# Retention ahead of two feed-forward layers: matmuls pinned in runs by tile form, q by chunk, one-piece decay and state update, and a first group ordered by weight tile

## The chip, the core and the metric

The kernel runs on one NeuronCore of a Trainium2 chip. The metric is the device time of one execution in microseconds, the median of three runs for the kernel before. The profiler's record of one execution (the trace) gives each engine's instructions: TensorE (PE for the matmuls, PEld for the loads of their stationary operand), VectorE (DVE), ScalarE (ACT), GpSimd (POOL) and SyncE (SP, which here only issues transfers).

## What is computed

Three stages run one after the other: a block-wise retention with a decaying state, a feed-forward layer with a mish activation, and one with elu. Input is q, k, v of shape (2, 8, 768, 64) in float32, and weights in float64.

```python
# retention, in blocks of 64 tokens (the kernel takes chunks of 128, which is the same sum)
intra = (qb @ kb.T * Dmask) @ vb               # Dmask[i, j] = lam ** (i - j) for i >= j, else 0
inter = (qb * lam_pow) @ kv_state
out   = intra + inter
kv_state = lam_block * kv_state + (kb * rev_pow).T @ vb
# layer 1: h = x @ w_in;  g = h * tanh(log(1 + exp(h)));  x = g @ w_out      (1536 tokens, 512 -> 2048 -> 512)
# layer 2: the same with g = where(h > 0, h, exp(h) - 1)
```

## The kernel before

**Retention.** The twelve chunks of 128 tokens are taken with the batch innermost: chunk n is batch n % 2, position c = n // 2. For each chunk `load` issues k, q and v on SP's queue; q comes for two chunks at once, as rows of two tokens (512 bytes), and only at even c. `transposes` turns k (four 128x128 transposes) and, at even c, q (eight) through PSUM, ACT copies them back, and GpSimd makes `q2` (q times the decay since the chunk's start) and `kd` (k times the decay to its end). `scores` multiplies k by q, per head, on half of the array's rows (64x128), the two heads of a pair into two PSUM tiles `sc`, each a buffer of its own. `decay` multiplies each by the mask `dm` on VectorE. `outputs` adds, pair by pair in `o`, one 128x128 matmul of the block-diagonal state `sbd` with `q2` (L276) and two 128x64 matmuls of v with the decayed scores (L280); then eight 128x64 matmuls make the state's increment `st` (L293), and VectorE updates `sd` in four instructions (L304). The result is split in a rounded part `xh` (ACT, L288) and a rest `xl` (VectorE, L311). The loop does transposes and scores of chunk n and then decay and outputs of chunk n-1. Each float32 matmul that is no transpose stands in the trace as two records.

**Feed-forward.** A step is (layer, group of four weight tiles, 512 tokens): `mm_in` forms h with 12 matmuls of 128x512 for each weight tile (L356), `mm_out` forms y with 12 for each of four column blocks (L398). There are 24 steps, 2304 such matmuls' worth of work in all. Each weight tile comes as float64 bits and is turned into two parts by eight VectorE instructions (L89 to L132) and one copy on ACT; a table by chunk and by unit says when. In the first group all eight tiles are made during the retention, after chunks 4 to 11. The order of units is in (step s), then out (step s-1).

**Order.** The program text gives priorities; a scheduler with a model of the times puts each engine's instructions in the order in which they are issued, and it may take a later matmul ahead of an earlier one that it believes not ready. At run time each engine keeps its order. `psH` holds two PSUM buffers for h that exist during the retention; the other buffers of the feed-forward part (`psL`, `psY`, `acc`, `g`) take the retention's memory after its end (`open_late`). The step of the first 512 tokens is written inside the retention's scope (`at_end`), so its 48 matmuls can be taken early, as far as the two buffers allow.

Of the kernel before, what the change touches and what calls it, by code (L numbers as in the profile page):

```python
# [8 lines left out]
F32 = mybir.dt.float32  # L9
# [3 lines left out]
AF = mybir.ActivationFunctionType  # L13
# [5 lines left out]
def kernel(  # L19
# [13 lines left out]
    P = 128  # L33
# [101 lines left out]

    def retention(after_chunk, at_end):
        es = ExitStack()
        cst = es.enter_context(tc.tile_pool(name="cst", bufs=1))
        io = es.enter_context(tc.tile_pool(name="io", bufs=3))
# [7 lines left out]
        nat, tr, sc, am, qT2 = {}, {}, {}, {}, {}  # L147


        def load(n, parts=1):  # L150
            b, c = chunks[n]
            for nm, src in (("k", k), ("q", q), ("v", v)):
                if nm != "q":
                    shape, rows, form = [P, H, D], slice(c * P, (c + 1) * P), "h p d -> p h d"
                elif c % 2 == 0:
                    shape, rows = [P, H, 2 * D], slice(c * P, (c + 2) * P)
                    form = "h (p x) d -> p h (x d)"
                else:
                    continue
                t = io.tile(shape, F32, tag=nm + "n", name=nm + "n", bufs=2 if nm == "q" else 3)  # L160
                for y in range(parts):
                    hs = slice(y * H // parts, (y + 1) * H // parts)
                    s = src[b, hs, rows, :]
                    nc.sync.dma_start(
                        out=t[:, hs], in_=s.rearrange(form, **({"x": 2} if nm == "q" else {}))
                    )
                nat[n, nm] = t
# [45 lines left out]
        def transposes(n):  # L213
            b, c = chunks[n]
            kn = nat[n, "k"]
            ps = psT.tile([P, PR, P], F32, tag="T", name="kTp")
            for r in range(PR):
                nc.tensor.transpose(  # L218
                    ps[:, r], kn[:, 2 * r:2 * r + 2].rearrange("p h d -> p (h d)"), ident
                )  # L220
            kT = wk.tile([P, PR, P], F32, tag="kT", name="kT")
            nc.scalar.activation(out=kT, in_=ps, func=AF.Copy)
            if c % 2 == 0:
                qn = nat[n, "q"]
                qT2[b] = wk.tile([P, PR, 2 * P], F32, tag="qT", name="qT")
                for hh in range(2):
                    ps = psT.tile([P, PR, P], F32, tag="T", name="qTp")
                    for r in range(PR):
                        nc.tensor.transpose(ps[:, r], qn[:, 2 * r + hh], ident)  # L229
                    for x in range(2):  # L230
                        dst = qT2[b][hh * D:(hh + 1) * D].rearrange("p r (i x) -> p r i x", x=2)
                        nc.scalar.activation(  # L232
                            out=dst[:, :, :, x], in_=ps[x * D:(x + 1) * D], func=AF.Copy
                        )
            qT = qT2[b][:, :, (c % 2) * P:(c % 2 + 1) * P]
            q2 = None
            if c > 0:
                q2 = wk.tile([P, PR, P], F32, tag="q2", name="q2", bufs=1)
                nc.gpsimd.tensor_tensor(out=q2, in0=qT, in1=lq, op=ALU.mult)
            kd = None  # L240
            if c < NCH - 1:
                kd = wk.tile([P, H, D], F32, tag="kd", name="kd")
                nc.gpsimd.tensor_tensor(  # L243
                    out=kd, in0=kn, in1=dm[:, :, P - 1:P].to_broadcast([P, H, D]), op=ALU.mult
                )
            tr[n] = (kT, qT, q2, kd)

        def scores(n):
            kT, qT, _, _ = tr[n]
            ps = [psS.tile([P, PR, P], F32, tag="sc", name=f"sc{hh}") for hh in range(2)]  # L250
            for r in range(PR):
                for hh in range(2):
                    rows = slice(hh * D, (hh + 1) * D)
                    nc.tensor.matmul(  # L254
                        ps[hh][:, r], lhsT=kT[rows, r], rhs=qT[rows, r], start=True, stop=True
                    )
            sc[n] = ps

        def decay(n):
            a = wk.tile([P, 2, PR, P], F32, tag="am", name="am")  # L260
            for hh, ps in enumerate(sc.pop(n)):
                nc.vector.tensor_tensor(
                    out=a[:, hh], in0=ps, in1=dm.rearrange("p (r t) i -> p r t i", t=2)[:, :, hh],
                    op=ALU.mult,
                )
            am[n] = a

        def outputs(n):
            b, c = chunks[n]
            _, _, q2, kd = tr.pop(n)  # L270
# [3 lines left out]
            for r in range(PR):  # L274
                if c > 0:
                    nc.tensor.matmul(  # L276
                        o[:, r], lhsT=sbd[b][:, r], rhs=q2[:, r], start=True, stop=False
                    )
                for hh in range(2):
                    nc.tensor.matmul(  # L280
                        o[hh * D:(hh + 1) * D, r],
                        lhsT=vn[:, 2 * r + hh],
                        rhs=a[:, hh, r],
                        start=(c == 0),
                        stop=True,
                    )
            t, col = divmod(n * P, TB)
            nc.scalar.activation(out=xh[t][:, :, col:col + P], in_=o, func=AF.Copy)  # L288
            if c < NCH - 1:
                st = psO.tile([P, PR, D], F32, tag="st", name="st")  # L290
                for r in range(PR):
                    for hh in range(2):
                        nc.tensor.matmul(  # L293
                            st[hh * D:(hh + 1) * D, r],
                            lhsT=kd[:, 2 * r + hh],
                            rhs=vn[:, 2 * r + hh],
                            start=True,
                            stop=True,
                        )
                if c == 0:  # L300
                    nc.vector.tensor_copy(sd[b], st)
                else:
                    for r in range(PR):
                        nc.vector.scalar_tensor_tensor(  # L304
                            out=sd[b][:, r], in0=sd[b][:, r], scalar=lc[:, r], in1=st[:, r],
                            op0=ALU.mult, op1=ALU.add,
                        )
# [30 lines left out]
    def open_late():  # L338
        def pool(name, **kw):
            return ctx.enter_context(tc.tile_pool(name=name, reuse_waits="tile", **kw))  # L340

        late["y"] = pool("yp", bufs=1)
        late["g"] = pool("gp", bufs=8)
# [79 lines left out]
    def mm_in_all(s):  # L423
        for i in range(G):
            h = mm_in(s, i)
            (mish, elu)[steps[s][0]](s, i, h)
            if late:
                split_g(s, i)
            weights_at(s * 2 * G + i)

    def mm_out_all(s):
        for d in range(KD):
            if s > 0:

                parts = 2 if s == NS and d == KD - 1 else 1
                for x in range(parts):
                    cols = slice(x * TB // parts, (x + 1) * TB // parts)
                    flush(s - 1, d, cols, mm_out(s - 1, d, cols))
            weights_at(s * 2 * G + G + d)
# [3 lines left out]
    CHUNKS = B * NCH  # L443
    FIRST = (4, 5, 6, 7, 8, 9, 10, 11)
    LATER = (0, 3, 6, 9, 12, 14, 16, 20)
    at = {}
    for n in range(NW):
        g, i = divmod(n, PG)
        at.setdefault(FIRST[i] - CHUNKS if g == 0 else LATER[i] + (g - 1) * 24, []).append(n)

    def weights_at(u):
        for n in at.get(u, ()):
            if n == 0:
                for m in range(AHEAD):
                    w_load(m)
            w_guard(n)
            w_bits(n)
            w_split(n)
            w_load(n + AHEAD)

    retention(lambda n: weights_at(n - CHUNKS), lambda: mm_in_all(0))
    open_late()
    for i in range(G):
        split_g(0, i)
    for s in range(NS + 1):
        if 0 < s < NS:
            mm_in_all(s)
        mm_out_all(s)
# [32 lines left out]
```

## Time and profile before

| what | us |
|---|---|
| median of three runs | 616.55 (616.34 to 617.07) |
| the profiled execution, its time | 617.07 |
| the profiled execution, its span (first to last instruction) | 615.3 |
| PE busy | 605.3 |
| VectorE busy | 446.6 |
| ScalarE busy | 227.7 |
| GpSimd busy | 172.1 |

The span is what the trace shows; 1.8 us of the execution's time lie around it. A busy time is the union of an engine's instructions, whose ends are modelled on PE; how fast PE goes is read from the distance between the starts of its instructions, not from the busy share.

### The profile page before, as it was taken

The numbers are of one execution on the slowest core, as the hardware profiler recorded it, in microseconds if no ns is written. First come the engines' busy times: TensorE is split into PE (matmuls) and PEld (weight loads), VectorE is DVE, ScalarE is ACT, GpSimd is POOL, SyncE is SP. The second block draws the span as 40 slices with busy tenths as digits, with TensorE's granted clock in tenths as the row PEclk, the third lists the DMA queues.
The fourth block names the chain that finished last, engine by engine and source line by source line (L and its number), as shares of the span: only waits on it lengthen the run. The fifth ranks groups of instructions, "written<-read, shape, count | busy, mean of one in ns | idle before, by whom it ended". The sixth has DMA issues, their size and how long they took to land.

```text
span 615.3 us, 7925 instructions
## 1 busy us (share of the span) xinstructions
PE 605.3 (98%) x3036; PEld 495.6 (81%) x3036; DVE 446.6 (73%) x751; ACT 227.7 (37%) x387; POOL 172.1 (28%) x126
## 2 busy tenths in 40 slices
PE   6999999999999999999999999999999999999997
PEld 4877777788888888888888888888888888888886
DVE  5798996499906993499549995899569965952222
ACT  3464732431323233223233534533343443254130
POOL 5143411730333143123313123213311421232130
PEclk9999999999999999999999999999999999999999
DMA  8985433023300321033202221132203320000112
GB/s 200 266 219 139 122 118 103 2 68 103 102 1 15 105 90 67 1 102 93 79 1 68 69 74 64 35 103 68 69 12 93 103 68 1 0 2 0 69 39 99
DMA packets 54807, 46.66 MB, mean 76 GB/s; under 512 B 26480, under 2 KB 49264, under 8 KB 54768
## 3 DMA queue, kind: packets, MB, share of 16 engines
q1 hardware_dynamic: 54624, 46.14, 25.6%
q8 instruction: 24, 0.39, 0.3%
q14 instruction: 15, 0.12, 0.1%
q10 hardware_dynamic: 144, 0.00, 0.0%
HBM read 43.00 MB, written 3.15 MB: 75 GB/s over the span
## 4 chain that ended last, share of the span: by engine, by line
PE 96%; DVE 1%; ACT 1%; DMA 0%; issue 0%; POOL 0%; ACTq 0%
PE y L398 42%; PE h L356 42%; PE sc L254 4%; PE o L280 3%; PE o L276 2%; PE st L293 1%; PE kTp L218 1%; PE qTp L229 1%; DMA lam_b<-in_lam_dram 0%; ACT qT L232 0%; DVE dm L187 0%; ACT L374 0%; DVE m L89 0%; POOL kd L243 0%; DVE step L185 0%
## 5 line engine op out<-in xcount | busy, mean ns | idle before, releaser
L356 PE MATMUL h<-xh,w 128*128 128x512 f32 x768 | 241.6, 390 | 0.7 <-ACT xh L288 0.7
L366 POOL TENSOR_TENSOR g<-g,g 128x512 fp32r<-128x512 f32 x96 | 137.5, 1438 | 351.9 <-ACT g L365 332.2
L356 PEld LDWEIGHTS h<-xh,w 128*128 128x128 f32 x768 | 143.8, 188 | 30.8 <-ACT xh L288 0.9
L356 PE MATMUL h<-xl,w 128*128 128x512 f32 x384 | 149.6, 389 | 0.0
L398 PE MATMUL y<-g,w 128*128 128x512 f32 x576 | 132.7, 389 | 0.0
L398 PE MATMUL y<-w,g 128*128 128x512 f32 (+1 forms) x588 | 132.5, 385 | 0.0
L398 PEld LDWEIGHTS y<-w,g 128*128 128x128 f32 x588 | 108.9, 188 | 22.0
L398 PEld LDWEIGHTS y<-g,w 128*128 128x128 f32 x576 | 108.1, 188 | 22.6 <-ACT g L365 0.2
L410 DVE TENSOR_TENSOR acc<-acc,y 128x512 f32<-128x512 f32 (+1 forms) x73 | 48.7, 673 | 75.3 <-PE y L398 75.3
L131 ACT ACTIVATE w<-m 128x512 fp32r<-128x512 f32 x64 | 40.5, 633 | 166.9 <-DVE m L120 114.3
L356 PEld LDWEIGHTS h<-xl,w 128*128 128x128 f32 x384 | 72.1, 188 | 14.8
L365 ACT ACTIVATE g<-g 128x512 fp32r<-128x512 f32 x96 | 60.0, 631 | 52.9 <-DVE g L383 51.5
L383 DVE SCALAR_TENSOR_TENSOR g<-e,h 128x512 f32<-128x512 f32 x48 | 32.7, 682 | 41.5 <-ACT e L381 26.9
L132 DVE TENSOR_TENSOR w<-m,w 128x512 fp32r<-128x512 f32 x64 | 45.7, 715 | 20.5 <-ACT w L131 20.3
L116 DVE SCALAR_TENSOR_TENSOR u<-raw,u 128x512 f32<-128x512 uint32 x64 | 57.2, 894 | 0.3
L108 DVE SCALAR_TENSOR_TENSOR b<-raw,b 128x512 int32<-128x512 int32 x64 | 50.0, 781 | 0.6
L120 DVE TENSOR_TENSOR m<-b,u 128x512 f32<-128x512 f32 x64 | 48.3, 754 | 0.3
L374 ACT ACTIVATE g<-h 128x512 f32<-128x512 f32 x48 | 28.1, 588 | 41.7 <-PE h L356 28.6
L104 DVE TENSOR_SCALAR b<-m 128x512 int32<-128x512 int32 x64 | 38.9, 609 | 0.3
L380 ACT ACTIVATE e<-h 128x512 f32<-128x512 f32 x48 | 28.2, 587 | 29.1 <-PE h L356 29.1
L112 DVE TENSOR_SCALAR u<-b 128x512 int32<-128x512 int32 x64 | 36.5, 570 | 0.3
L93 DVE TENSOR_SCALAR m<-m 128x512 f32<-128x512 f32 x64 | 35.7, 558 | 0.3
(44 smaller groups left out, 367.5 us busy)
## 6 DMA issues: line engine op xcount, KB each, us to landing
raw<-in_moe_w_in_dram SPq DMA_DIRECT2D x32, 512.0 KB, 3.7
raw<-in_moe_w_out_dram SPq DMA_DIRECT2D x32, 512.0 KB, 3.3
kn<-in_k_dram SPq DMA_DIRECT2D x11, 256.0 KB, 4.6
vn<-in_v_dram SPq DMA_DIRECT2D x11, 256.0 KB, 3.8
out_dram<-acc SPq DMA_DIRECT2D x11, 256.0 KB, 2.0
qn<-in_q_dram SPq DMA_DIRECT2D x5, 512.0 KB, 5.8
qn<-in_q_dram SPq DMA_DIRECT2D x2, 256.0 KB, 3.9
kn<-in_k_dram SPq DMA_DIRECT2D x2, 128.0 KB, 3.2
```

Source lines behind the costliest of these rows:

```text
L104: nc.vector.tensor_scalar(out=b, in0=m, scalar1=3, scalar2=0x3FFFFFF8, op0=ALU.logical_shift_left, op1=ALU.bitwise_and,)
L108: nc.vector.scalar_tensor_tensor(out=b, in0=hw, scalar=-0x40000000, in1=b, op0=ALU.bitwise_and, op1=ALU.bitwise_or)
L112: nc.vector.tensor_scalar(out=u, in0=b, scalar1=-0x800000, scalar2=None, op0=ALU.bitwise_and)
L116: nc.vector.scalar_tensor_tensor(out=u.bitcast(F32), in0=lw, scalar=2.0 ** -52, in1=u.bitcast(F32), op0=ALU.mult, op1=ALU.mult,)
L120: nc.vector.tensor_tensor(out=m.bitcast(F32), in0=b.bitcast(F32), in1=u.bitcast(F32), op=ALU.add)
L131: nc.scalar.activation(out=w[:, 0], in_=f, func=AF.Copy)
L132: nc.vector.tensor_tensor(out=w[:, 1], in0=f, in1=w[:, 0].bitcast(F32), op=ALU.subtract)
L356: nc.tensor.matmul(h, lhsT=lt, rhs=rt, start=(kk == 0 and n == 0), stop=(kk == KD - 1 and n == 2),)
L365: nc.scalar.activation(out=gg[:, 0], in_=g, func=AF.Copy)
L366: nc.gpsimd.tensor_tensor(out=gg[:, 1], in0=g, in1=gg[:, 0].bitcast(F32), op=ALU.subtract)
L398: nc.tensor.matmul(y, lhsT=lt, rhs=rt, start=(i == 0 and n == 0), stop=(i == G - 1 and n == 2),)
L410: nc.vector.tensor_tensor(out=dst, in0=dst, in1=y, op=ALU.add)
```

## The change

- The matmuls and transposes of the retention are pinned: each is kept behind the matmul written before it. The loop now does, for chunk n: load of n+3, transposes of n+1, scores of n, decay of n, outputs and state of n-1.
- q is loaded for each chunk like k (rows of 256 bytes), transposed in four transposes and copied back by one ACT instruction; k, q and v have four buffers instead of two or three.
- The two score tiles become one tile over two PSUM banks, with one buffer, and `decay` is one VectorE instruction over 1024 columns.
- In `outputs` the state's term is made by two 128x64 matmuls for a pair of heads instead of one 128x128, all of them ahead of the eight with v.
- The state update is two VectorE instructions instead of four.
- The first group goes by weight tile over all three blocks of 512 tokens (12 units "in", then out of step 0 and 1, then as before). Two of its units stand in the retention's scope. Only three weight tiles are made during the retention; the others follow in units 0 to 8, the second group's in units 10 to 24. The first four weight loads are issued after chunks 3, 5, 7 and 9. The buffers of g go from 8 to 12.

```diff
-        psS = es.enter_context(tc.tile_pool(name="psS", bufs=2, space=PSUM))
+        psS = es.enter_context(tc.tile_pool(name="psS", bufs=1, space=PSUM))
+        def pe(ins):
+            tc.keep_in_program_order(ins)
...
-                t = io.tile(shape, F32, tag=nm + "n", name=nm + "n", bufs=2 if nm == "q" else 3)
+                t = io.tile([P, H, D], F32, tag=nm + "n", name=nm + "n")
...
-            ps = [psS.tile([P, PR, P], F32, tag="sc", name=f"sc{hh}") for hh in range(2)]
+            ps = psS.tile([P, 2, PR, P], F32, tag="sc", name="sc")
...
-            for hh, ps in enumerate(sc.pop(n)):
-                nc.vector.tensor_tensor(
-                    out=a[:, hh], in0=ps, in1=dm.rearrange("p (r t) i -> p r t i", t=2)[:, :, hh],
-                    op=ALU.mult,
-                )
+            nc.vector.tensor_tensor(
+                out=a, in0=sc.pop(n), in1=dm.rearrange("p (r t) i -> p t r i", t=2), op=ALU.mult
+            )
...
+            if c > 0:
+                terms += [
+                    (r, hh, sbd[b][:, r, hh * D:(hh + 1) * D], q2[:, r])
+                    for r in range(PR) for hh in range(2)
+                ]
+            terms += [
+                (r, hh, vn[:, 2 * r + hh], a[:, hh, r]) for r in range(PR) for hh in range(2)
+            ]
+            for x, (r, hh, lt, rt) in enumerate(terms):
+                pe(nc.tensor.matmul(
+                    o[hh * D:(hh + 1) * D, r], lhsT=lt, rhs=rt,
+                    start=x < 2, stop=x >= len(terms) - 2, skip_group_check=True,
+                ))
...
-                    for r in range(PR):
-                        nc.vector.scalar_tensor_tensor(
-                            out=sd[b][:, r], in0=sd[b][:, r], scalar=lc[:, r], in1=st[:, r],
-                            op0=ALU.mult, op1=ALU.add,
-                        )
+                    nc.vector.tensor_tensor(
+                        out=sd[b], in0=sd[b], in1=lc.to_broadcast([P, PR, D]), op=ALU.mult
+                    )
+                    nc.vector.tensor_tensor(out=sd[b], in0=sd[b], in1=st, op=ALU.add)
...
+        transposes(0)
         for n in range(NC + 1):
+            load(n + 3)
+            if n + 1 < NC:
+                transposes(n + 1)
             if n < NC:
-                transposes(n)
-                if 0 < n and n + 2 < NC:
-                    load(n + 2)
                 scores(n)
+                decay(n)
             if n > 0:
-                decay(n - 1)
                 outputs(n - 1)
-                after_chunk(n - 1)
+            after_chunk(n)
...
+    seq = [("in", t, i) for i in range(G) for t in range(NTB)]
+    tail = [("out", 0), ("out", 1)]
+    for s in range(NTB, NS):
+        tail += [("in", s), ("out", s - 1)]
...
-    FIRST = (4, 5, 6, 7, 8, 9, 10, 11)
-    LATER = (0, 3, 6, 9, 12, 14, 16, 20)
+    FIRST = (4 - CHUNKS, 7 - CHUNKS, 10 - CHUNKS, 0, 2, 4, 6, 8)
+    SECOND = (10, 12, 14, 16, 18, 20, 22, 24)
+    LATER = (24, 27, 30, 33, 36, 38, 40, 44)
...
+    LOAD = {3 - CHUNKS: 0, 5 - CHUNKS: 1, 7 - CHUNKS: 2, 9 - CHUNKS: 3}
...
+    EARLY = 2
```

## Rows read from the trace of the kernel before

**Rows 1.** The page's chain that ended last: shares of the span by line.
```profile
PE y L398 42%; PE h L356 42%; PE sc L254 4%; PE o L280 3%; PE o L276 2%; PE st L293 1%; PE kTp L218 1%; PE qTp L229 1%; DMA lam_b<-in_lam_dram 0%; ACT qT L232 0%; DVE dm L187 0%; ACT L374 0%; DVE m L89 0%; POOL kd L243 0%; DVE step L185 0%
```

**Rows 2.** Windows: busy us (instructions) by engine, granted clock, DMA share, GB/s.
```profile
4.00:20.70 16.70, 15.02 (x88) 11.62 (x88) 9.25 (x16) 7.84 (x14) 5.60 (x6) 1.00 1.05 265
20.70:110.20 89.50, 89.32 (x729) 68.82 (x728) 77.98 (x158) 39.72 (x70) 25.53 (x15) 1.00 0.54 147
...
111.00:616.00 505.00, 500.84 (x2220) 415.01 (x2220) 358.88 (x576) 178.10 (x301) 137.53 (x96) 1.00 0.18 57
...
200.00:300.00 100.00, 100.00 (x443) 82.84 (x442) 81.81 (x135) 29.05 (x50) 25.61 (x17) 1.00 0.25 77
```

**Rows 3.** The same for L356 alone: PE, PEld, clock, DMA.
```profile
0.00:110.20 110.20, 24.02 (x96) 17.42 (x96) 1.00 0.62 163
```

**Rows 4.** Timeline of PE (start, us, line), the feed-forward's start and end.
```profile
110.85 0.73 PE L356 MATMUL h<-xh,w 128*128 128x512 f32 x2 [0.70 <-ACT xh L288]
...
597.70 14.14 PE L398 MATMUL y<-w,g 128*128 128x512 f32 x73
```

**Rows 5.** Timeline of PE, one chunk in the middle of the retention.
```profile
55.67 0.49 PE L276 MATMUL o<-q,sbd 128*128 128x128 f32 x2
56.09 0.44 PE L280 MATMUL o<-am,vn 128*64 128x128 f32 x4
56.46 0.49 PE L276 MATMUL o<-q,sbd 128*128 128x128 f32 x2
...
58.03 1.16 PE L254 MATMUL sc<-qT,kT 64*128 64x128 f32 x16
59.12 0.69 PE L293 MATMUL st<-vn,kd 128*64 128x64 f32 x16
59.74 1.09 PE L229 MATMUL qTp<-ident,qn 128*128 128x128 f32 x8
60.59 0.47 PE L356 MATMUL h<-xh,w 128*128 128x512 f32 x1
```

**Rows 6.** Timeline of PE, scores of one chunk in two halves.
```profile
48.96 1.16 PE L254 MATMUL sc<-qT,kT 64*128 64x128 f32 x8
50.05 0.69 PE L293 MATMUL st<-vn,kd 128*64 128x64 f32 x16
50.66 1.16 PE L254 MATMUL sc<-qT,kT 64*128 64x128 f32 x8
```

**Rows 7.** Timeline of PE, a long run of 128x64 matmuls.
```profile
27.47 1.09 PE L280 MATMUL o<-am,vn 128*64 128x128 f32 x14
28.49 0.66 PE L218 MATMUL kTp<-ident,kn 128*128 128x128 f32 x4
```

**Rows 8.** Timeline of PE, half-runs of scores early and later.
```profile
10.00 2.07 PE L254 MATMUL sc<-qT,kT 64*128 64x128 f32 x8
...
20.73 1.16 PE L254 MATMUL sc<-qT,kT 64*128 64x128 f32 x8
```

**Rows 9.** Groups of instructions to 110.2 us, VectorE: busy, mean ns, idle before.
```profile
L262 DVE TENSOR_TENSOR am<-sc,dm 128x512 f32<-128x512 f32 x24 | 16.2, 680 | 4.9 <-PE sc L254 4.9
...
L304 DVE SCALAR_TENSOR_TENSOR sd<-sd,lq,st 128x64 f32<-128x64 f32 x32 | 6.7, 268 | 0.0
```

**Rows 10.** Timeline of VectorE: a weight instruction beside GpSimd, and a 256-column one.
```profile
118.28 1.40 DVE L89 TENSOR_SCALAR m<-raw 128x512 int32<-128x512 int32 x1
...
610.44 0.42 DVE L410 TENSOR_TENSOR acc<-acc,y 128x256 f32<-128x256 f32 x1 [0.74 <-PE y L398]
```

**Rows 11.** Groups to 123 us, ScalarE and GpSimd.
```profile
L239 POOL TENSOR_TENSOR q<-qT,lq 128x512 f32<-128x512 f32 x10 | 19.5, 1955 | 49.9 <-PE o L276 49.1 <-DVE lq L202 0.7
L243 POOL TENSOR_TENSOR kd<-kn,dm 128x512 f32<-128x512 f32 x10 | 11.4, 1148 | 19.6 <-DMA kn<-in_k_dram 8.2 <-PE st L293 6.6 <-DVE lq L202 3.7
...
L288 ACT ACTIVATE xh<-o 128x512 fp32r<-128x512 f32 x12 | 7.2, 598 | 14.3 <-PE o L280 14.1
```

**Rows 12.** Transfers from 3 to 12 us: packets and rate.
```profile
DMA packets 6742, 2.21 MB, mean 245 GB/s; under 512 B 4694, under 2 KB 6742, under 8 KB 6742
```

More of the change, by code (lines that the diff above doesn't have):

```diff
@@ L146, in retention @@
         NC = len(chunks)
-        nat, tr, sc, am, qT2 = {}, {}, {}, {}, {}
+        nat, tr, sc, am, qkd = {}, {}, {}, {}, {}
+        def pe(ins):
+            tc.keep_in_program_order(ins)
         def load(n, parts=1):
+            if n >= NC:
+                return
             b, c = chunks[n]
             for nm, src in (("k", k), ("q", q), ("v", v)):
[L153 to L159, printed above, removed]
-                t = io.tile(shape, F32, tag=nm + "n", name=nm + "n", bufs=2 if nm == "q" else 3)
-                for y in range(parts):
-                    hs = slice(y * H // parts, (y + 1) * H // parts)
-                    s = src[b, hs, rows, :]
+                t = io.tile([P, H, D], F32, tag=nm + "n", name=nm + "n")
+                np_ = 1 if nm == "v" else parts
+                for y in range(np_):
+                    hs = slice(y * H // np_, (y + 1) * H // np_)
                     nc.sync.dma_start(
-                        out=t[:, hs], in_=s.rearrange(form, **({"x": 2} if nm == "q" else {}))
+                        out=t[:, hs],
+                        in_=src[b, hs, c * P:(c + 1) * P, :].rearrange("h p d -> p h d"),
                     )
@@ L235, in transposes @@
[L235 to L244, printed above, removed]
-                )
@@ L246, in transposes @@
-            tr[n] = (kT, qT, q2, kd)
+            out = []
+            for nm in ("k", "q"):
+                x = nat[n, nm]
+                ps = psT.tile([P, PR, P], F32, tag="T", name=nm + "Tp")
+                for r in range(PR):
+                    pe(nc.tensor.transpose(
+                        ps[:, r], x[:, 2 * r:2 * r + 2].rearrange("p h d -> p (h d)"), ident
+                    ))
+                t = wk.tile([P, PR, P], F32, tag=nm + "T", name=nm + "T")
+                nc.scalar.activation(out=t, in_=ps, func=AF.Copy)
+                out.append(t)
@@ new lines, in transposes @@
+            tr[n] = out
+            q2 = kd = None
+            if c > 0:
+                q2 = wk.tile([P, PR, P], F32, tag="q2", name="q2")
+                nc.gpsimd.tensor_tensor(out=q2, in0=out[1], in1=lq, op=ALU.mult)
+            if c < NCH - 1:
+                kd = wk.tile([P, H, D], F32, tag="kd", name="kd", bufs=3)
+                nc.gpsimd.tensor_tensor(
+                    out=kd, in0=nat[n, "k"], in1=dm[:, :, P - 1:P].to_broadcast([P, H, D]),
+                    op=ALU.mult,
+                )
@@ L253, in scores @@
                     rows = slice(hh * D, (hh + 1) * D)
-                    nc.tensor.matmul(
-                        ps[hh][:, r], lhsT=kT[rows, r], rhs=qT[rows, r], start=True, stop=True
-                    )
+                    pe(nc.tensor.matmul(
+                        ps[:, hh, r], lhsT=kT[rows, r], rhs=qT[rows, r], start=True, stop=True
+                    ))
             sc[n] = ps
@@ L273, in outputs @@
             o = psO.tile([P, PR, P], F32, tag="o", name="o")
[L274 to L286, printed above, removed]
+            terms = []
+            if c > 0:
+                terms += [
[6 more added lines that the diff above has]
+            for x, (r, hh, lt, rt) in enumerate(terms):
+                pe(nc.tensor.matmul(
+                    o[hh * D:(hh + 1) * D, r], lhsT=lt, rhs=rt,
+                    start=x < 2, stop=x >= len(terms) - 2, skip_group_check=True,
+                ))
             t, col = divmod(n * P, TB)
@@ L292, in outputs @@
                     for hh in range(2):
-                        nc.tensor.matmul(
+                        pe(nc.tensor.matmul(
                             st[hh * D:(hh + 1) * D, r],
@@ L342, in open_late @@
         late["y"] = pool("yp", bufs=1)
-        late["g"] = pool("gp", bufs=8)
+        late["g"] = pool("gp", bufs=12)
         late["psH"] = pool("psL", bufs=2, space=PSUM)
@@ L421, in flush, with unit @@
             nc.sync.dma_start(out=out[r0:r0 + P, cols], in_=dst)
[L423 to L426, printed above, removed]
-            if late:
[L428 to L443, printed above, removed]
-    FIRST = (4, 5, 6, 7, 8, 9, 10, 11)
-    LATER = (0, 3, 6, 9, 12, 14, 16, 20)
+    seq = [("in", t, i) for i in range(G) for t in range(NTB)]
+    HEAD = len(seq)
+    tail = [("out", 0), ("out", 1)]
+    for s in range(NTB, NS):
+        tail += [("in", s), ("out", s - 1)]
+    tail.append(("out", NS - 1))
+    for kind, s in tail:
+        seq += [(kind, s, x) for x in range(G if kind == "in" else KD)]
+    def unit(u):
+        kind, s, x = seq[u]
+        if kind == "in":
+            (mish, elu)[steps[s][0]](s, x, mm_in(s, x))
+            if late:
+                split_g(s, x)
+        else:
+            parts = 2 if u == len(seq) - 1 else 1
+            for y in range(parts):
+                cols = slice(y * TB // parts, (y + 1) * TB // parts)
+                flush(s, x, cols, mm_out(s, x, cols))
+    CHUNKS = B * NCH + 1
     at = {}
+    FIRST = (4 - CHUNKS, 7 - CHUNKS, 10 - CHUNKS, 0, 2, 4, 6, 8)
+    SECOND = (10, 12, 14, 16, 18, 20, 22, 24)
+    LATER = (24, 27, 30, 33, 36, 38, 40, 44)
     for n in range(NW):
         g, i = divmod(n, PG)
-        at.setdefault(FIRST[i] - CHUNKS if g == 0 else LATER[i] + (g - 1) * 24, []).append(n)
+        u = (FIRST, SECOND)[g][i] if g < 2 else LATER[i] + (g - 2) * 24
+        at.setdefault(u, []).append(n)
+    LOAD = {3 - CHUNKS: 0, 5 - CHUNKS: 1, 7 - CHUNKS: 2, 9 - CHUNKS: 3}
     def weights_at(u):
+        if u in LOAD:
+            w_load(LOAD[u])
         for n in at.get(u, ()):
-            if n == 0:
-                for m in range(AHEAD):
-                    w_load(m)
             w_guard(n)
@@ L459, in weights_at, with first_units @@
             w_load(n + AHEAD)
-    retention(lambda n: weights_at(n - CHUNKS), lambda: mm_in_all(0))
-    open_late()
[L463 to L468, printed above, removed]
+    EARLY = 2
+    def first_units():
+        for u in range(EARLY):
+            unit(u)
+            weights_at(u)
+    retention(lambda n: weights_at(n - CHUNKS), first_units)
+    open_late()
+    for u in range(EARLY):
+        split_g(seq[u][1], seq[u][2])
+    for u in range(EARLY, len(seq)):
+        unit(u)
+        weights_at(u)
 _INS = ["q", "k", "v", "lam", "moe_w_in", "moe_w_out", "moe2_w_in", "moe2_w_out"]
```

29 lines of the change are left out of this document (5 added, 24 removed).

## The prediction

> **What bounds the kernel now.** I read the chain that ended last first: its lines on PE add up to 96% of the span [rows 1]. So TensorE's own order of work is the clock of this kernel, and other engines count only where they make it wait. The windows split it [rows 2]: from 111.0 us on PE does nothing but the feed-forward layers. Their last matmul ends at 597.70 + 14.14 = 611.84 us [rows 4], so 500.84 us hold 2220 records, of which 24 are halves (the last block is split in two): 2208 whole ones, **0.2268 us** each. By 110.2 us 96 others were done [rows 3], 2304 in all: 2304 x 0.2268 = 522.6 us is feed-forward work that the change keeps. The other 611.84 - 522.6 = **89.2 us** are the start, the retention and its stalls. The change can only win there, and can lose there or where the first group of weights is late.
>
> That these 89 us are PE's work, not waiting, is seen in the same windows: from 20.7 to 110.2 us PE is busy 89.32 of 89.50 us, VectorE 77.98 [rows 2]. Busy on PE is modelled, so I price runs by the distance of their starts.
>
> **The change part by part, on PE.** All prices are of one chunk, from 20.7 us on. Before that a run of 8 score records takes 2.07 us, from then on 1.16 [rows 8]: the lower of TensorE's levels (1.2 GHz) and then the higher (2.4 GHz), though the granted-clock column prints 1.00 for both [rows 2].
>
> Outputs. A pair of heads takes 56.46 - 55.67 = 0.79 us before (one state matmul, two of v, thus two changes of form), four pairs 3.14 us [rows 5]. A long run of 14 records of 128x64 takes 28.49 - 27.47 = 1.02 us, four of them 56.46 - 56.09 = 0.37 [rows 5, 7]: (1.02 - 0.37)/10 = 0.065 us a record and 0.37 - 4 x 0.065 = 0.11 us for the change of form. After: 16 records for the state and 16 for v in one form, 32 x 0.065 + 0.11 = **2.19 us**, 0.95 less, in ten chunks.
>
> Scores. The scheduler issues one head of each pair (8 records) apart from the other: 50.05 - 48.96 = 1.09 us, twice a chunk [rows 6]; where both stand together, 16 records take 59.12 - 58.03 = 1.09 us as well [rows 5]. Two halves of the rows work at once if they are neighbours in the order. One tile and pinning make them neighbours: **1.09 us** a chunk. Seven of twelve chunks were split (14 runs of 8 stand alone in the timeline).
>
> State and transposes. 16 state records take 59.74 - 59.12 = 0.62 us; behind the outputs there is no change of form, so 0.62 - 0.11 = **0.51**. Eight transposes take 60.59 - 59.74 = **0.85** [rows 5]; k and q now stand together in each chunk.
>
> Sum: 2.19 + 1.09 + 0.51 + 0.85 = 4.64 us a chunk, 55.7 for twelve; the two first chunks have no state term (16 x 0.065 = 1.04 each), the two last no state update (0.51 each): **52.6 us** at the higher level.
>
> Start. The first transposes wait for k at 4 us as before. q's first half is 128 KB instead of 256, so I let PE be dense from 7.5 us and the clock rise at 20.7 as before (1 us either way). By then 0.85 + (20.7 - 7.5)/2 = 7.4 us of the 52.6 are done; the retention ends at 20.7 + 45.2 = **66 us** without stalls.
>
> **What can make PE wait.** The two units in the retention's scope (24 matmuls) may fill holes, but the pinned ones can no longer change places, so each late input now costs.
>
> Scores need the one score buffer free: the wait is behind `decay`, one VectorE instruction of 1024 columns. From 256 columns (0.42) and 512 (0.68) [rows 9, 10] it is about 0.68 + 2 x 0.26 = 1.20 us; meanwhile PE has outputs, state and transposes, 3.55 us. Outputs need `o` free: `xh` on ACT 0.60 [rows 11], then `xl` on VectorE 0.68 by the same width, maybe behind a weight instruction that GpSimd holds up, 1.40 [rows 10]: 2.7 us, against 0.51 + 0.85 + 1.09 = 2.45 us of other work. So 0 to 0.25 us, eleven times, and a little more where the scheduler's order on VectorE is unlucky: bounds 0 to 6, I take **2 us**, near the lower, since only three weight tiles lie in this stretch.
>
> VectorE's own edits cost PE nothing: the decay 1.20 instead of 2 x 0.68, the state 2 x 0.42 instead of 4 x 0.268 [rows 9, 10]; if GpSimd holds the new SBUF multiply, up to 1.40, a chunk's 2.9 us of VectorE work still fits in 4.64. ACT loses four half copies per two chunks and gains one whole one per chunk. GpSimd has 1.96 + 1.15 = 3.1 us a chunk [rows 11], also under 4.64.
>
> Loads. On SP the load of v for chunk n+3 now waits for the state matmuls of chunk n-1, and k and q of n+4 and a weight load are queued behind it; their user, the transposes of n+4, comes two rounds (9 us) later. The first four weight loads are spread over chunks 3 to 9 instead of standing in one block in the first 20 us. A chunk is 768 KB; from 3 to 12 us, with 4694 of 6742 packets under 512 bytes, the transfers ran at 245 GB/s [rows 12]: 3.2 us a chunk, with half a weight load (512 KB) 4.3, under 4.64, so nothing; 3.5 for a chunk all in short packets is my upper bound from the same row.
>
> The end of the retention. PE waited 0.70 us for the last `xh` [rows 4]; other h matmuls then covered the wait for `xl`, another 0.68. Now only unit 2 stands there: **1.4 us**, 0.7 if a unit was kept back for it.
>
> Weights. Tiles come later: 8 VectorE instructions each, and 77.98/158 = 0.49 us per instruction in the retention, 81.81/100 x 100/135 = 0.61 in the layers [rows 2], so 3.9 to 4.9 us a tile; 11 where each meets GpSimd as the worst row does (1.40). The twelfth tile is due at unit 23, at 66 + 23 x 12 x 0.2268 = 129 us; the first can start near 26 us, when its load has landed. In these 103 us VectorE owes 8 chunks x 2.7 = 22, 8 flushes x 0.68 = 5, and 12 tiles: 86 us at 4.9 a tile. It fits; due time and work meet at 6.3 a tile. I take **1 us** for one tile that comes late, bounds 0 to 19 (7.9 us a tile, halfway to the worst).
>
> **Sum.** 66 + 522.6 + 2 + 1.4 + 1 = 593.0 us to the last matmul, 615.3 - 611.84 = 3.5 behind it as before: span 596.5, and the time is 1.8 longer than the span (617.07 against 615.3): 598.3. The median stands 0.5 under the profiled execution: **597.8 us**, 18.8 less.
>
> **The rivals.**
>
> VectorE becomes the bound (chance 0.19). In the first twelve units GpSimd runs one instruction per unit against about half that before, and the weights' VectorE instructions wait for it. At 7 us a tile the twelfth is 22 + 5 + 84 - 103 = 8 us late instead of 1: **605 us**, 602 to 613. For it: the 1.40 us row. Against it: a mean of 0.61 in the layers.
>
> Transfers bind (0.04). Rows 12 say no. The Trainium skill, "DMA: Bandwidth & Descriptors", its table of properties, wants at least 512 bytes for line rate, which speaks against q in rows of 256. With q's third of a chunk at half the speed of rows 12, 4.3 us a chunk, and a weight load (512 KB, 2.1 us) in every second round, the queue needs 5.3 against 4.64 for about six chunks: **602 us**.
>
> The state matmuls in two halves don't overlap (0.05): records alone cost (1.09 - 0.11)/8 = 0.12 us [rows 6], 16 of them 0.9 more a chunk, in ten chunks 9: **607 us**. Against it: the run of rows 7 overlaps in the same form.
>
> It doesn't do what it says (0.06): the 24 unpinned matmuls are put one by one between pinned ones, two changes of form each, 24 x 2 x 0.11 = 5 us: **603 us**.
>
> Slower (0.06): the pinned order leaves gaps that grow by the clock. If PE waits in each round, TensorE goes back to 1.2 GHz, a chunk costs 9.3 us instead of 4.64, and if that lasts to the end the retention ends near 111 us: **643 us**. It decides against the change once more than 18.8 us of the 45.2 run at the lower level. Rows 8 show that the level is low while the start is thin. The Trainium skill, "TensorE: Matmul & The Clock Gate", on oscillation in real kernels, says that pauses between bursts of matmuls bring the lower clock back; no row here shows it after 20.7 us. Against it: the longest wait found above is far under a microsecond.
>
> **How the numbers follow.** The forecast (592 to 602 us) has 0.60: no stall at all gives 593.4, the bounds of the small stalls 602. With VectorE bound, transfers, half overlap and stray matmuls (602 to 613) it is 0.94. For 8 in 10 I go from 590 (clock up 3 us earlier, no stalls) to 610. About 0.2% is what can be told from no change. Faster 0.92, the same 0.02 (VectorE worse than its rival's range), slower 0.06.
>
> **What would show it.** Score runs of 16 records 1.09 us apart; output runs of 32 records in some 2.2; a last retention matmul near 68 us plus what early h matmuls take (up to 5.4); no PE gap over 1 us up to unit 23; VectorE's idle time there above zero. Wrong would be: gaps on PE behind `xl`, `am` or a weight tile of over 8 us in sum, or matmuls after 25 us that take twice their time.

## The result and the profile after

The changed kernel takes **621.14 us** (median of five runs, 618.8 to 621.23) against 616.35 for the kernel before beside it: a ratio of 1.0068, with a 95% interval of 1.0049 to 1.0087. It is 0.7% slower; 597.8 us had been forecast, 18.8 less than before, in a range of 590 to 610. The profiled execution has a span of 617.0 us and is the fastest of the five (618.80 us), so the rows below show rather less than the median's loss.

What the change does to TensorE's own work came out near the forecast. The timeline of PE of the changed kernel (start, us, line) for one chunk, to be held against [rows 5 to 7]:

```profile
60.30 1.16 PE L246 MATMUL sc<-qT,kT 64*128 64x128 f32 x16
61.39 1.09 PE L275 MATMUL o<-q,sbd 128*64 128x128 f32 x16
62.31 1.04 PE L275 MATMUL o<-am,vn 128*64 128x128 f32 x16
63.19 0.64 PE L285 MATMUL st<-vn,kd 128*64 128x64 f32 x16
63.75 0.66 PE L221 MATMUL kTp<-ident,kn 128*128 128x128 f32 x4
64.25 0.60 PE L221 MATMUL qTp<-ident,qn 128*128 128x128 f32 x4
64.78 1.16 PE L246 MATMUL sc<-qT,kT 64*128 64x128 f32 x16
```

The starts give 1.09 us for the scores, 1.80 for the outputs, 0.56 for the state and 1.03 for the transposes: 4.48 us a chunk where 4.64 was forecast. What is new is waiting. The waits of PE from 20 to 150 us in the changed kernel (in us, times, longest):

```profile
PE o L275 <- DVE xl L302: 9.1, 5, 4.0
PE sc L246 <- DVE am L253: 5.7, 3, 4.6
PE y L390 <- DVE acc L400: 4.1, 1, 4.1
PE h L348 <- ACT xh L280: 0.7, 1, 0.7
```

Before, PE had waited only the 0.70 us of [rows 4] there. All but 0.7 of these 19.6 us are waits for VectorE. The windows of the changed kernel (busy us and instructions of PE, PEld, DVE, ACT, POOL; granted clock; DMA share; GB/s) show what goes with them:

```profile
20.00:30.00 10.00, 5.41 (x59) 4.95 (x59) 8.21 (x15) 2.77 (x6) 2.57 (x3) 0.83 1.16 290
30.00:40.00 10.00, 7.66 (x115) 6.60 (x111) 10.00 (x16) 4.05 (x8) 4.41 (x4) 1.00 1.06 231
...
50.00:60.00 10.00, 7.73 (x105) 7.22 (x102) 10.00 (x19) 3.12 (x7) 4.91 (x4) 0.83 0.62 144
...
90.00:100.00 10.00, 9.31 (x48) 7.52 (x45) 9.58 (x15) 2.26 (x4) 2.97 (x2) 0.66 0.33 107
...
130.00:140.00 10.00, 5.85 (x18) 4.41 (x17) 9.97 (x17) 3.50 (x6) 2.85 (x2) 0.73 0.32 105
```

VectorE has almost no free time (of its 1.79 us without work in the first stretch, 1.65 are the end of a wait for a load). TensorE's granted clock is below 1.00 in the stretches of three of the four waits of over 2 us; the other ends at 89.41 us, and the clock is down in the stretch after it. What VectorE was doing is in the timeline of the first of them. Its queue, and the row of PE that waited:

```profile
21.65 0.60 DVE L89 TENSOR_SCALAR m<-raw 128x512 int32<-128x512 int32 x1 [2.70 <-DMA raw<-in_moe_w_in_dram]
22.29 0.43 DVE L93 TENSOR_SCALAR m<-m 128x512 f32<-128x512 f32 x1
22.75 0.43 DVE L104 TENSOR_SCALAR b<-m 128x512 int32<-128x512 int32 x1
23.21 0.69 DVE L108 SCALAR_TENSOR_TENSOR b<-raw,b 128x512 int32<-128x512 int32 x1
23.93 0.43 DVE L112 TENSOR_SCALAR u<-b 128x512 int32<-128x512 int32 x1
24.28 1.22 DVE L253 TENSOR_TENSOR am<-sc,dm 128x1024 f32<-128x1024 f32 x1
...
25.55 2.08 PE L246 MATMUL sc<-qT,kT 64*128 64x128 f32 x16 [4.59 <-DVE am L253]
```

Five instructions of the first weight tile stand in VectorE's queue ahead of the decay (L253), and the first of them waits 2.70 us for its load. The decay comes late, the single score buffer stays taken, and the pinned scores stand for 4.59 us. Then they take 2.08 us, nearly twice the 1.16 of the chunk above: the lower of the clock's levels, 1.2 GHz instead of 2.4. The load itself had been moved. In the timeline of SP's queue four weight loads (2 MB) go out within 5 us, not after chunks 3, 5, 7 and 9 as the program text has them:

```profile
16.19 1.10 SPq L76 DMA_DIRECT2D raw<-in_moe_w_in_dram  x1
...
18.12 1.13 SPq L82 DMA_DIRECT2D raw<-in_moe_w_out_dram  x1
19.30 0.43 SPq L76 DMA_DIRECT2D raw<-in_moe_w_in_dram  x1
...
20.63 2.33 SPq L76 DMA_DIRECT2D raw<-in_moe_w_in_dram  x1
```

And the weight tiles went with them. The window of the last instruction of a tile (L132: busy us and count; clock; DMA share; GB/s) counts the tiles that VectorE finished in the changed kernel; by the text three belong into the retention:

```profile
20.00:80.00 60.00, 5.64 (x7) 0.94 0.78 189
```

**Theories.** *Q (VectorE's queue):* the table of weight tiles gives only priorities; the scheduler fills VectorE and SP with weight work far ahead of its need, in front of the decay and `xl`, and the pinned matmuls, which can't change places, wait. *P (pinning):* it is the pinning that makes the loss, whatever VectorE does. *T (VectorE's sum):* VectorE has too much work for the shorter retention in any order. *F (first group):* the loss is in the new order of the first group. *D (transfers):* it is the crowded DMA queues and the one wait behind them.

### The profile page after: what moved, and what is told of

It is laid out like the page before. It is cut to its first block, busy times and chain, and to the rows that moved or that the text cites. A ratio compares the mean times of both kernels' runs of the same rounds, so it can differ in the third digit from the quotient of the medians.

```text
span 617.0 us, 8058 instructions
## 1 busy us (share of the span) xinstructions
PE 587.6 (95%) x3116; PEld 487.7 (79%) x3116; DVE 447.3 (72%) x723; ACT 218.6 (35%) x375; POOL 166.4 (27%) x126
## 4 chain that ended last, share of the span: by engine, by line
PE 80%; DVE 14%; issue 2%; DMA 2%; ACT 1%; SPq 1%; ACTq 0%
PE y L390 41%; PE h L348 38%; DVE b L108 2%; DVE m L89 2%; DVE am L253 2%; DVE m L93 1%; DVE u L116 1%; DVE m L120 1%; SPq L164 1%; DVE b L104 1%; DVE u L112 1%; DMA raw<-in_moe_w_in_dram 1%; DVE sd L295 1%; DMA qn<-in_q_dram 1%; DVE xl L302 1%
## 5 line engine op out<-in xcount | busy, mean ns | idle before, releaser
L390 PE MATMUL y<-g,w 128*128 128x512 f32 x576 | 135.7, 394 | 4.1 <-DVE acc L400 4.1
L390 PEld LDWEIGHTS y<-g,w 128*128 128x128 f32 x576 | 109.7, 191 | 27.8 <-DVE acc L400 4.6
L116 DVE SCALAR_TENSOR_TENSOR u<-raw,u 128x512 f32<-128x512 uint32 x64 | 58.9, 921 | 0.2
L132 DVE TENSOR_TENSOR w<-m,w 128x512 fp32r<-128x512 f32 x64 | 44.6, 697 | 16.8 <-ACT w L131 16.6
L120 DVE TENSOR_TENSOR m<-b,u 128x512 f32<-128x512 f32 x64 | 49.9, 780 | 0.3
L104 DVE TENSOR_SCALAR b<-m 128x512 int32<-128x512 int32 x64 | 37.2, 582 | 0.4
```

Source lines behind the costliest of these rows:

```text
L104: nc.vector.tensor_scalar(out=b, in0=m, scalar1=3, scalar2=0x3FFFFFF8, op0=ALU.logical_shift_left, op1=ALU.bitwise_and,)
L116: nc.vector.scalar_tensor_tensor(out=u.bitcast(F32), in0=lw, scalar=2.0 ** -52, in1=u.bitcast(F32), op0=ALU.mult, op1=ALU.mult,)
L120: nc.vector.tensor_tensor(out=m.bitcast(F32), in0=b.bitcast(F32), in1=u.bitcast(F32), op=ALU.add)
L132: nc.vector.tensor_tensor(out=w[:, 1], in0=f, in1=w[:, 0].bitcast(F32), op=ALU.subtract)
L390: nc.tensor.matmul(y, lhsT=lt, rhs=rt, start=(i == 0 and n == 0), stop=(i == G - 1 and n == 2),)
```

## The experiments

### e1: the matmuls not pinned

```diff
-            tc.keep_in_program_order(ins)
+            return ins
```

> The changed kernel without the pinning: the scheduler may change the order of the retention's matmuls again, all else as changed. Theory Q (VectorE's queue: weight instructions that the scheduler put ahead of decay and xl make the pinned-or-not TensorE wait): the waits for am and xl stay, 614 to 622 us. Rival P (the pinning itself is what leaves TensorE idle, because nothing can fill a gap): 595 to 606 us, gaps behind am and xl under 5 us in sum.

Measured: 607.36 us, ratio 0.9851 (0.9834 to 0.9867). Neither theory as written: 14 us faster than the changed kernel, 1.4 above the 595 to 606 of P, whose other sign, waits under 5 us, is there. VectorE takes seven tiles by 80 us here too, but TensorE waits for `xl` and `am` only 3.1 us; Q's waits that stay are refuted. The waits of PE from 20 to 150 us that are over 1 us:

```profile
PE y L390 <- DVE acc L400: 4.3, 1, 4.3
PE h L348 <- ACT xh L280: 2.2, 1, 2.2
PE o L275 <- DVE xl L302: 1.9, 2, 1.1
PE kTp L221 <- DMA kn<-in_k_dram: 1.4, 1, 1.4
PE sc L246 <- DVE am L253: 1.2, 2, 0.8
```

So the early weight work alone does not make the loss in the retention; it takes the pinned order to turn it into waits. The wait of 4.3 us for a flushed PSUM buffer in the first group (`acc`) is untouched.

### e2: VectorE's weight work in its written order

```diff
-        nc.vector.tensor_scalar(
+        first = nc.vector.tensor_scalar(
             out=m.bitcast(I32), in0=raw[n][:, :, 1], scalar1=1, scalar2=1,
             op0=ALU.logical_shift_left, op1=ALU.logical_shift_right,
         )
+        if n < 2 * PG:
+            tc.keep_in_program_order(first)
```

> The changed kernel with one instruction more pinned: the first VectorE instruction of each of the first sixteen weight tiles stays behind the VectorE instructions written before it, so that only three tiles lie in the retention. Theory Q: the waits of TensorE for am and xl (some 15 us in the changed kernel) fall under 5 us, the last retention matmul comes near 72 us, the time is 596 to 606 us. Rival P (pinned matmuls): 616 to 622, waits as before. Rival T (VectorE has too much work in sum, whatever its order): the waits move from the retention to the first groups, behind weight tiles, 612 to 622 us.

Measured: 607.04 us, 0.9841 (0.9819 to 0.9864), 1 us above Q's stretch. The matmuls are as pinned as in the changed kernel, and three tiles instead of seven are done by 80 us. The waits of PE from 20 to 150 us that are over 1 us:

```profile
PE y L392 <- ACT w L133: 3.9, 2, 3.1
PE qTp L223 <- DMA qn<-in_q_dram: 3.2, 1, 3.2
PE h L350 <- ACT g L368: 2.1, 1, 2.1
PE o L277 <- DVE xl L304: 1.1, 1, 1.1
```

As Q says, the waits for `am` and `xl` are down from 14.8 us to 1.1. T has its share: 3.9 us of waits behind weight tiles (`w`) appear in the first group. And the early loads, which this kernel leaves where they were, show: the transposes wait 3.2 us for q.

### e3: five of VectorE's eight weight instructions left out

```diff
-        b = cv.tile([P, DM], I32, tag="b", name="b")
+        if n >= 2 * PG:
+            b = cv.tile([P, DM], I32, tag="b", name="b")
...
```

> The changed kernel with five of the eight VectorE instructions of the first sixteen weight tiles left out (those that put the mantissa together), so that VectorE has less to do and the values are not the reference's. Theories Q and T: the waits for am and xl shrink to about 3/8, 600 to 610 us. Rival P: no change, 616 to 622.

Measured: 604.13 us, 0.9798 (0.9779 to 0.9818). VectorE is busy 51.94 us between 20 and 100 us instead of 76.37. The waits for `xl` fall to 1.3 us, but the first wait for `am` stays, 4.33 us: VectorE has time enough, and still stands behind a load with the decay in its queue. So order counts apart from the sum of the work. The time itself (two runs) is what Q and T both expected and does not part them.

### e4: the old first group behind the new retention

```diff
-    seq = [("in", t, i) for i in range(G) for t in range(NTB)]
+    seq = []
+    for s in range(NS + 1):
+        seq += [("in", s, i) if s < NS else None for i in range(G)]
+        seq += [("out", s - 1, d) if s > 0 else None for d in range(KD)]
...
-    EARLY = 2
+    EARLY = G
```

> The changed retention with the first group of the kernel before: four units of the first 512 tokens in the retention's scope, eight weight tiles made after chunks 4 to 11, the old table. Theory Q: the scheduler takes nearly as many weight tiles into the retention in both, so the waits for am and xl stay: 612 to 624 us. Rival F (the loss comes from the new order of the first group): 596 to 606.

Measured: 606.67 us, 0.9834 (0.9815 to 0.9853). The time falls between the two expectations. In the retention TensorE still waits 8.9 us for `am` and 3.0 for `xl`, as Q says; from 100 us on the trace shows no wait of TensorE. Against the changed kernel 19.6 - 11.9 = 7.7 us of waits are gone, 4.8 of them behind the retention (`acc` and the last `xh`) and 2.9 in it; that the clock brings the rest of the 14 us is an inference. The time lies 0.7 us above F's stretch and 5 under Q's: F has a part, by the time a large one, and Q's waits are there as well.

### e5: the weight loads in their written order

The DMA of a weight tile is pinned on SP's queue for the first sixteen tiles, as the instruction in e2.

> The changed kernel with one thing more pinned: the loads of the first sixteen weight tiles stay on SP's queue behind the loads written before them (in the changed kernel four of them, 2 MB, go out between 16 and 21 us, ahead of most of chunks 4 and 5). Theory Q (weight work taken too early, and with it VectorE's queue): without early loads there are no early weight instructions; the wait of 4.6 us at 21 us goes, the later waits for xl and am fall under 5 us in sum: 600 to 608 us. Rival D (only the crowded transfers and that one wait matter, the rest is VectorE's queue all the same): some 7 us with the clock's loss behind it, 612 to 616.

Measured: 617.45 us, 1.0006 (0.999 to 1.0023): 4 us under the changed kernel, above what Q expected and above D's stretch too. The wait at 21 us is gone, but a like one has come at 35 us. The rows of PE with waits of over 3 us from 20 us on:

```profile
38.40 2.08 PE L248 MATMUL sc<-qT,kT 64*128 64x128 f32 x16 [3.41 <-DVE am L255]
...
83.92 1.98 PE L277 MATMUL o<-q,sbd 128*64 128x128 f32 x16 [3.55 <-DVE xl L304]
...
132.71 13.13 PE L392 MATMUL y<-g,w 128*128 128x512 f32 x48 [5.62 <-DVE acc L402]
```

Five tiles instead of seven are done by 80 us, and they still stand ahead of what TensorE waits for. D falls as the whole cause, and Q has to be read as the order of VectorE's queue, not as the hour of the loads.

### e6: both in their written order

e2 and e5 together.

> Loads as in e5 and the first VectorE instruction of each tile as in e2. Theory Q: in the retention no wait over 1.5 us and no loss of the clock; the last retention matmul at 70 to 75 us with the 24 early ones; waits behind weight tiles in the first group stay as in e2 (some 7 us), since three tiles in the retention are too few: 598 to 604 us.

Measured: 611.27 us, 0.9914 (0.9886 to 0.9942), 4 us slower than e2 alone and outside the expectation. The wait for q is gone, but the first tile's load now goes out so late that VectorE stands 5.66 us for it, with the decay behind, and TensorE 4.0 us; the waits behind weight tiles in the first group are those of e2. A written order keeps an error of the table as well.

### e7: both in order, and five tiles in the retention

```diff
-    FIRST = (4 - CHUNKS, 7 - CHUNKS, 10 - CHUNKS, 0, 2, 4, 6, 8)
+    FIRST = (4 - CHUNKS, 6 - CHUNKS, 8 - CHUNKS, 10 - CHUNKS, 11 - CHUNKS, 1, 4, 7)
-    LOAD = {3 - CHUNKS: 0, 5 - CHUNKS: 1, 7 - CHUNKS: 2, 9 - CHUNKS: 3}
+    LOAD = {2 - CHUNKS: 0, 4 - CHUNKS: 1, 6 - CHUNKS: 2, 7 - CHUNKS: 3}
```

> As e6, with five weight tiles made after chunks 4, 6, 8, 10 and 11 instead of three, the other three after units 1, 4 and 7. If VectorE has room in the retention once its order is right, the waits behind weight tiles in the first group fall under 3 us and none come in the retention: 595 to 601 us. Rival T (VectorE's work in sum): the waits come back in the retention, no faster than e6.

Measured: **596.16 us**, 0.9674 (0.9658 to 0.969). From 80 us on TensorE waits for no weight tile. VectorE's work over retention and first group is the same in sum (four tiles, not seven, are done by 80 us), so T falls: there is room, in the right order and at the right places. One wait is left, 2.87 us at 37.5 us, for a decay behind an instruction that waited 2.0 us for the first load.

### e8: two buffers for the outputs' PSUM tile

`o` gets a second buffer, taken from the early h, which leaves one early unit.

> The changed kernel with two buffers for the outputs' PSUM tile o and one for the early h (so one early unit instead of two), all else as changed. Theory Q: a late xl no longer stops the next outputs, so most of the 9 us of waits for xl go, those for am (5.7 us) stay: 609 to 615 us. If it is faster than 605 the single buffer is the main cause, not the order.

Measured: 615.33 us, 0.9986 (0.9975 to 0.9996), just above the expected stretch and some 6 us under the changed kernel, so the single buffer is not the main cause. The waits for `xl` are gone, and those for `am` have grown from 5.7 to 10.4 us: with another buffer TensorE runs into the next late instruction of the same queue. The run has one early unit less as well.

### e9: e7 without pinned matmuls

> e7 without the pinning of the retention's matmuls (VectorE's weight instructions and the weight loads stay in order, five tiles). Theory Q says that pinned matmuls were harmed only by VectorE's order: with that order right, taking the pins away gains nothing, 595 to 602 us. Rival P (pinning itself costs): under 593.

Measured: 595.71 us, 0.9666 (0.965 to 0.9682), e7 had 596.16. With VectorE in order and e7's table, pinning costs nothing and brings nothing; P falls as a cause of its own. Whether pinning brings something with e10's table below was not run.

### e10: e7 with the first load after chunk 1

```diff
-    LOAD = {2 - CHUNKS: 0, 4 - CHUNKS: 1, 6 - CHUNKS: 2, 7 - CHUNKS: 3}
+    LOAD = {1 - CHUNKS: 0, 4 - CHUNKS: 1, 6 - CHUNKS: 2, 7 - CHUNKS: 3}
```

> e7 with the first weight load written after chunk 1 instead of 2, since e7 shows VectorE waiting 2.0 us for it with the decay queued behind, and TensorE 2.9 us behind that, with a lower clock in the two windows that follow. If that load is the cause, the wait goes and the clock stays up: 590 to 593.5 us. If the wait only moves (another load is late instead): 595 to 597.

Measured: **592.51 us**, 0.9626 (0.9595 to 0.9656), the fastest of all, 24 us under the kernel before; three of its four runs lie between 592.0 and 592.8. The profiled execution is the fourth (596.14 us), and its waits of PE from 20 to 150 us are:

```profile
PE sc L250 <- DVE am L257: 2.9, 1, 2.9
PE o L279 <- DVE xl L306: 1.1, 1, 1.1
PE h L352 <- ACT xh L284: 0.7, 1, 0.7
```

VectorE no longer waits for the first load. In this execution it waits for the second one, with the decay queued behind:

```profile
43.69 0.43 DVE L91 TENSOR_SCALAR m<-raw 128x512 int32<-128x512 int32 x1 [3.12 <-DMA raw<-in_moe_w_in_dram]
```

So the profiled execution, with 596.14 us, is the second case of the expectation (the wait only moves, 595 to 597), and the median is the first; that the other three had no such wait is only inferred from their times.

### e11: the kernel before with its weight work in order

> The kernel before with the same two pins for the first sixteen weight tiles (loads and first VectorE instructions), nothing else. Its TensorE waits for nothing between 21 and 110 us, so theory Q gives it no gain: 614 to 620 us. A gain of over 5 us would say that the order of the weight work costs the kernel before as well, by other ways than waits.

Measured: 619.52 us, 1.0044 (1.0028 to 1.0061): no gain, and a loss of 0.4%. Two tiles instead of seven are done by 80 us. The kernel before takes its seven without a wait of TensorE.

### e12: the old first group, with weight work in order

> e4 (new retention, first group and tables of the kernel before) with both pins for the weight work. Here eight tiles belong into the retention, where VectorE has room for some five: if VectorE's work per stretch is the next bound, the waits for am and xl stay between 5 and 12 us, 602 to 608 us. If order alone decides: 594 to 599, as e7, and the first group by weight tile brings nothing.

Measured: 603.36 us, 0.978 (0.9758 to 0.9802), 3 us better than e4 and 7 worse than e7. TensorE waits 6.0 us for `xl`, 5.4 of it at once at 45 us, with a granted clock of 0.66 in that window, and 2.9 us for a weight tile. Time and waits (8.9 us) lie where the first case of the expectation put them, but the longest wait has another cause. The old table writes the first four loads directly ahead of the first tile's instructions, and VectorE stands for the load, with `xl` queued behind:

```profile
43.30 0.43 DVE L91 TENSOR_SCALAR m<-raw 128x512 int32<-128x512 int32 x1 [5.99 <-DMA raw<-in_moe_w_in_dram]
...
45.60 1.97 PE L279 MATMUL o<-q,sbd 128*64 128x128 f32 x16 [5.45 <-DVE xl L306]
```

As in e6 (5.66 us), that is the place of a load, and e7 had moved its loads. So the 7 us to e7 do not show that the first group by weight tile brings something.

## Why the prediction was wrong

**What held.** 89.2 us of start, retention and stalls were to fall to 70.4. The price of a chunk held in sum (4.48 us against 4.64), by misses that offset each other: 1.80 against 2.19 for the outputs, 0.56 against 0.51 for the state, 1.03 against 0.85 for the transposes. Two halves of rows and of columns do overlap in runs. The start was better than forecast. The clock was to rise at 20.7 us, as before, 1 us either way; in the changed kernel the same four transposes and the scores are at the price of the higher level some 8 us earlier:

```profile
8.34 1.09 PE L221 MATMUL kTp<-ident,kn 128*128 128x128 f32 x4 [1.75 <-DMA kn<-in_k_dram]
...
12.18 0.66 PE L221 MATMUL kTp<-ident,kn 128*128 128x128 f32 x4
...
13.68 1.16 PE L246 MATMUL sc<-qT,kT 64*128 64x128 f32 x16
```

e10 gives the sum back, in part by luck: its last matmul ends at 579.63 + 11.42 = 591.05 us, minus 522.6 leaves 68.4 us. But 4.7 us of these are waits, about the 4.4 that had been allowed, and some 1.5 us the clock behind the longest of them, so the work without stalls took less than the 66 us of the forecast.

The short rows of q do cost rate, but little. The window of the changed kernel from 3 to 12 us, as in [rows 12] and ahead of all weight loads:

```profile
3.00:12.00 9.00, 5.90 (x32) 4.08 (x32) 6.53 (x11) 2.39 (x4) 3.38 (x5) 1.00 1.19 225
```

That is 225 GB/s against the 245 of [rows 12]: 3.5 us a chunk, at the bound of 3.5 and under a chunk of PE. The Trainium skill, "DMA: Bandwidth & Descriptors", table of properties, has the direction right (at least 512 bytes for line rate); the half rate that was worked out beside it is not what these rows show.

**The step that failed** is in the part on what can make PE wait: the 2 us taken "near the lower, since only three weight tiles lie in this stretch", and with it that the "first four weight loads are spread over chunks 3 to 9". Both read the table as a timetable. It is a list of priorities, and the trace shows seven tiles by 80 us and four loads by 21 us. (Early matmuls of the feed-forward part were misread in the same way: 48 of them, not 24, stand before the last of the retention.) The kernel before takes its weight tiles early too, seven by 80 us, and TensorE did not wait for them there; the prediction had VectorE's row of [rows 2], busy 77.98 of 89.5 us, and drew only a price from it.

The terms: 2 us for waits of the retention (bounds 0 to 6) measured 14.8; 1 us for weights in the first group measured 4.1, and not behind a weight tile but behind a flush (`acc`) that stood behind weight instructions. With 0.7 for `xh`, where 1.4 had been taken, that is 19.6 of waits where 4.4 were forecast, 15.2 more. Both signs that the prediction had named for being wrong are there: over 8 us of such gaps, and matmuls after 25 us at twice their time. The last matmul ends at 594.81 + 18.90 = 613.71 us:

```profile
594.81 18.90 PE L390 MATMUL y<-w,g 128*128 128x512 f32 x94
```

So 613.71 - 522.6 = 91.1 us are not feed-forward work, 20.7 over the forecast. The 5.5 us beyond the waits are the difference of two misses. The sum had no term for a lower clock after the start, and by the distances of starts in the timeline the matmuls behind the four waits of over 2 us took 1.5, 1.6, 3.0 and 2.6 us longer than such runs do at the higher level, 8.7 us in all. (The windows grant 0.83, 0.83, 0.66, 0.73 and, from 140 to 150 us, 0.93: 10.2 us of clock are missing, part of them while PE stood idle.) Against that, the 66 us without stalls were 3 to 4 too many: 91.1 - 19.6 - 8.7 leaves 62.8 here, 68.4 - 4.7 - 1.5 leaves 62.2 in e10; the earlier rise of the clock and the cheaper chunk fit that. This split is worked out, not shown by a run of its own.

**The rivals.** The slower one had the mechanism (pinned order, gaps, and the clock behind them), with a chance of 0.06, because "the longest wait found above is far under a microsecond", which came from that step; its price was too high, since the clock came back each time. Before the granted clock fell to 0.83 between 20 and 30 us, PE had waited 4.59 us. With what the Trainium skill, "TensorE: Matmul & The Clock Gate", says on oscillation in real kernels (pauses between bursts bring the lower clock back) these rows agree. "VectorE becomes the bound" was named, but for the sum of its work after the retention; e7 and e9 show that the same sum fits, and e3 that the first wait stays with less of it: the place in the queue decides.

**Which part of the change loses.** Not one alone. The early weight work was there before and harmless (e11), pinning is harmless if VectorE is in order (e9), and each of three remedies by itself brings some 14 us (e1, e2, and the old first group in e4). The loss in the retention needs both: a queue in which weight work stands ahead of the decay and `xl`, and a matmul order that can't change when an input is late. The first group adds the wait for `acc` and what the clock loses with it; put the old one back and it goes (e4). Which of the two is better with the weight work in order stays open, since e12 differs from e7 in the place of its loads too. The one score buffer, at which the waits for `am` arise, was not varied. Why only one of e10's four runs took 4 us longer is left open.

## What to carry to other kernels

A table of due times in the program text is no timetable where a scheduler fills each engine's queue by what is ready: count in the trace how much of the work was done by when before pricing what stands beside it. If one engine's order is pinned, pin the work that shares a queue with its inputs too, and then place it by hand, loads first: the changed kernel, with only its matmuls pinned, is 0.7% slower than the one before, and with the weight work pinned too, two more tiles in the retention and the first four loads one or two chunks earlier it is 3.7% faster (e10). It was VectorE's order that mattered: without the pinned matmuls, at e7's places, it is still 3.3% faster (e9). Each of the four waits of over 2 us on TensorE in the changed kernel was paid twice, once idle and once at the lower clock.

## What was not expected of the hardware

TensorE lost its clock in the midst of dense work after waits of a few microseconds: after 4.59 us of waiting at 21 us and 2.27 us at 53 us the granted clock of the window is 0.83, and after 3.98 us at 85 us it is 0.66. The rows of PE in the changed kernel that end the second and the third:

```profile
55.33 1.27 PE L275 MATMUL o<-q,sbd 128*64 128x128 f32 x16 [2.27 <-DVE xl L302]
56.32 1.98 PE L275 MATMUL o<-am,vn 128*64 128x128 f32 x16
...
89.41 1.22 PE L275 MATMUL o<-q,sbd 128*64 128x128 f32 x16 [3.98 <-DVE xl L302]
90.35 1.98 PE L275 MATMUL o<-am,vn 128*64 128x128 f32 x16
```

In both the run with v takes 1.98 us, where it takes 1.04 in the chunk shown first: here the matmuls behind the wait run on at the higher level for about a microsecond, and then at the lower one. Behind the wait of 4.59 us they are at the lower one from the start (the row of 25.55 us above, 2.08 us).
